# Two store waits of SyncE moved from ahead of the program's closing barrier to behind it

## The chip, the cores and the metric

The kernel runs on one core of one Trainium2 chip. The metric is the device time of one execution in microseconds (us), lower is better. Each execution also gives its **span**, from the first to the last instruction of the program, rounded to 0.1 us. The time is longer than the span in every run here, by 1.24 to 2.17 us, so it also contains something outside the program. I take that to be the runtime's work around it. I call time minus span the **excess**. I call the stretch from the issue of the last store to the end of the span the **tail**.

## The reference, cut to what matters

```python
def _A_ref(x, k_cache, v_cache, wq, wo):        # 32 heads, 32768 keys each
    q = ...(x @ wq)...
    scores = einsum("bhqd,bhkd->bhqk", q, k_cache) * Dh ** -0.5
    o = einsum("bhqk,bhkd->bhqd", softmax(scores), v_cache)
    return ...o... @ wo                          # 512 values
def _B_ref(...):                                 # 8 kv heads, only the last 4096 keys; the same otherwise
    ...
return concatenate([a, b], axis=-1)              # (1, 1, 1024) bf16
```

One token attends over two caches. The kernel reads 570 MB and writes two rows of 1 KB. B's row is ready early, A's row is the last thing to be made.

## The kernel before: the parts concerned

Instructions are collected as a list per engine (`self.op(engine, ...)`) and emitted in one block. Leaving the block emits a barrier of all five engines. In the trace of the kernel before, the drains of TensorE, VectorE, ScalarE and SyncE there each update one semaphore, SyncE's last (its end: 1321.126 us). GpSimd's next record waits for that semaphore (1321.151) and its last one updates a second (1321.230); the records of the other four that wait for the second start at 1321.271 to 1321.283.

```python
def build(self):
    ...
    with nc.Block() as block:                    # line 101: its end is the closing barrier
        block.gpsimd(self.emit("pool"))
        block.vector(self.emit("dve"))
        block.scalar(self.emit("act"))
        block.sync(self.emit("sp"))
        block.tensor(self.emit("pe"))

def plan(self):
    ...                                          # loads, B, 32 heads of A, output weights
    self.emit_proj()
    for n in self.outsem:                        # SyncE's last instructions
        self.op("sp", lambda e, n=n: e.wait_ge(self.outsem[n], 16))

def emit_proj(self):
    ...
    self.op("sp", lambda e: e.dma_start(self.out[0, :, 512:1024], self.qrow[0:1, :])
            .then_inc(self.outsem["B"], 16), o)               # line 740, the first store
    ...
    self.op("sp", lambda e: e.dma_start(self.out[0, :, 0:512], self.out_sb[:, :])
            .then_inc(self.outsem["A"], 16), *done)           # line 755, the last store
```

A wait for a store is kept in every kernel here: the landing comes 1.09 us after the issue's start. What happens without a wait, no run shows. Each store has a semaphore of its own (`outsem`), and a wait is for its count of 16.

## Time and profile before

| kernel before | us |
|---|---|
| median of its first three runs (range) | 1323.31 (1323.26 to 1323.33) |
| span of the profiled run | 1321.3 |
| last output copy ends, on VectorE | 1319.76 |
| last store issued (start, end) | 1319.845, 1320.093 |
| landing of that store, as its semaphore's last update records it (the wait ends 17 ns after) | 1320.937 |
| end of the block's barrier, end of the span | 1321.334 |

The page and the views that lead there are shown in the prediction below. Times to the nanosecond are taken from the trace's own records of the same instructions, which the views round to 0.1 us. The records also hold each update of a semaphore.

### The profile page before, as it was taken

To read this page: it belongs to the slowest core of one execution; us is meant where nothing else is said; L and a number is where in the kernel's file an instruction comes from. 1 tells how busy PE (TensorE), PEld (TensorE's weight loads), DVE (VectorE), ACT (ScalarE), POOL (GpSimd) and SP (SyncE) were. 2 spreads that over 40 slices of the span, in tenths; PEclk is the share of its full clock that TensorE was granted. 3 is DMA by queue.
4 is the path that set the end of the run, shared out by engine and by line. 5 is a ranking of instruction groups with operands and counts; after the bars stand their busy time and mean duration, and the time that the engine had idled before them with its cause. 6 is when DMAs were issued, how large, how long until landed. Compare 5 with 4: busy or idle time off the path is not lost. (4 is left out here: it accounts for less than half of the span.)

```text
span 1321.3 us, 28784 instructions
## 1 busy us (share of the span) xinstructions
PE 967.9 (73%) x13243; PEld 675.8 (51%) x13243; DVE 752.0 (57%) x1341; ACT 55.2 (4%) x168; POOL 2.6 (0%) x22
## 2 busy tenths in 40 slices
PE   4675678776777878676787767678776777877787
PEld 3453445554444655444465544455554445555453
DVE  3663556665455666554566655466655556665563
ACT  0000000000000000000000000000000000000000
POOL 0000000000000000000000000000000000000000
PEclk8886888888789888878988887898878779887898
DMA  9999999999999999999999999999999999999998
GB/s 403 434 438 428 442 433 429 440 436 427 439 436 429 438 438 427 436 438 433 431 438 434 429 438 434 429 438 436 427 440 432 431 440 432 429 440 434 431 436 367
DMA packets 13359, 570.59 MB, mean 432 GB/s; under 512 B 1570, under 2 KB 1700, under 8 KB 2084
## 3 DMA queue, kind: packets, MB, share of 16 engines
q1 hardware_dynamic: 13060, 570.43, 99.8%
q8 instruction: 8, 0.13, 0.0%
q10 hardware_dynamic: 288, 0.00, 0.0%
q14 instruction: 3, 0.02, 0.0%
HBM read 570.43 MB, written 0.00 MB: 432 GB/s over the span
## 5 line engine op out<-in xcount | busy, mean ns | idle before, releaser
L557 DVE COPY kt<-psT 128x1024 bf16<-128x1024 bf16 x1056 | 655.6, 684 | 237.0 <-PE psT L553 235.2
L553 PE MATMUL psT<-ident,kbuf 128*128 128x128 bf16 x8448 | 580.6, 234 | 167.3 <-DMA kbuf<-in_A_k_cache_dram 152.9
L553 PEld LDWEIGHTS psT<-ident,kbuf 128*128 128x128 bf16 x8448 | 540.7, 106 | 259.8 <-DMA kbuf<-in_A_k_cache_dram 161.0
L656 PE MATMUL psACC<-vbuf,ptsb 128*4 128x512 bf16 (+1 forms) x2112 | 183.9, 524 | 22.8 <-ACT ptsb L631 22.0
L576 PE MATMUL psS<-kt,qw 128*32 128x512 bf16 x2048 | 158.3, 386 | 15.0 <-DVE kt L557 15.0
L670 DVE TENSOR_SCALAR oc_A<-psACC,hot_A 128x128 f32<-128x128 f32 x32 | 11.2, 351 | 248.5 <-PE psG L683 248.5
L656 PEld LDWEIGHTS psACC<-vbuf,ptsb 128*4 128x4 bf16 (+1 forms) x2112 | 59.7, 110 | 137.4 <-issue 89.6
L604 ACT ACTIVATE psb<-psS,nb_A 128x512 bf16<-128x512 f32 x32 | 22.0, 687 | 1165.5 <-DVE nb_A L603 1165.5
L576 PEld LDWEIGHTS psS<-kt,qw 128*32 128x32 bf16 x2048 | 34.1, 95 | 57.8 <-DVE kt L557 31.2
L683 PE MATMUL psG<-oc_A,hw 128*32 128x128 f32 (+1 forms) x128 | 19.3, 227 | 52.3 <-DVE oc_A L672 52.3
L683 PEld LDWEIGHTS psG<-oc_A,hw 128*32 128x32 f32 x128 | 11.4, 109 | 62.5 <-DVE oc_A L672 55.1
L628 PE MATMUL psPT<-ident,psb 128*128 128x128 bf16 x136 | 18.0, 275 | 34.0 <-ACT psb L604 34.0
L672 DVE SCALAR_TENSOR_TENSOR oc_A<-psACC,hot_A,oc_A 128x128 f32<-128x128 f32 x96 | 33.7, 351 | 3.4
L593 DVE TENSOR_REDUCE tr_in<-psS 128x1 f32<-128x512 f32 x34 | 23.5, 692 | 17.6 <-PE psS L576 17.6
L628 PEld LDWEIGHTS psPT<-ident,psb 128*128 128x128 bf16 x136 | 10.1, 117 | 37.0 <-ACT psb L604 36.7
L597 PE MATMUL psACC<-rows,tr_in 128*1 128x64 f32 x64 | 8.8, 220 | 25.6 <-DVE tr_in L593 25.6
L631 ACT ACTIVATE ptsb<-psPT 128x512 bf16<-128x512 bf16 x34 | 20.3, 597 | 31.0 <-PE psPT L628 31.0
L597 PEld LDWEIGHTS psACC<-rows,tr_in 128*1 128x1 f32 x64 | 2.7, 81 | 35.5 <-DVE tr_in L593 35.5
L601 PE MATMUL psACC<-mr_A,nscale 1*128 1x1 f32 x64 | 12.4, 260 | 9.8 <-DVE mr_A L600 9.8
L601 PEld LDWEIGHTS psACC<-mr_A,nscale 1*128 1x128 f32 x64 | 9.7, 188 | 15.8 <-DVE mr_A L600 15.8
L603 DVE COPY nb_A<-psACC 128x1 f32<-128x1 f32 x32 | 5.0, 157 | 15.3 <-PE psACC L601 15.3
L495 PE MATMUL psACC<-vbuf,x_B 128*2 128x512 bf16 x32 | 3.6, 627 | 13.7 <-DMA x_B<-in_B_x_dram 13.7
(82 smaller groups left out, 76.0 us busy)
## 6 DMA issues: line engine op xcount, KB each, us to landing
kbuf<-in_A_k_cache_dram SPq DMA_DIRECT2D x4, 4096.0 KB, 22.4
kbuf<-in_B_k_cache_dram SPq DMA_DIRECT2D x2, 4096.0 KB, 31.8
vbuf<-in_B_v_cache_dram SPq DMA_DIRECT2D x2, 4096.0 KB, 24.7
vbuf<-in_B_wq_dram SPq DMA_DIRECT2D x1, 4096.0 KB, 12.7
vbuf<-in_A_wq_dram SPq DMA_DIRECT2D x1, 4096.0 KB, 32.2
kbuf<-in_B_wo_dram SPq DMA_DIRECT2D x2, 2048.0 KB, 33.6
kbuf<-in_A_wo_dram SPq DMA_DIRECT2D x1, 1408.0 KB, 28.0
kbuf<-in_A_wo_dram SPq DMA_DIRECT2D x1, 1024.0 KB, 30.1
```

Source lines behind the costliest of these rows:

```text
L553: inst = e.transpose(T[:, 128 * k:128 * k + 128], src[:, DH * k:DH * k + DH], self.ident[:, :])
L557: self.copies.append(self.op("dve", lambda v: v.tensor_copy(KT[:, :], T[:, :]), o, to="pe"))
L576: inst = e.matmul(self.S[32 * c:32 * c + 32, :], lhsT=win, rhs=self.kt[(bb + c // 2) % NKT][:, 512 * (c % 2):512 * (c % 2) + 512], start=b ...
L593: o = dve(lambda v: v.reduce_max(tr["in"][:, 0:1], self.S[:, :], axis=AXX), self.sdone, self.k_pool, to="pe" if name == "A" else None)
L597: o = self.op("pe", lambda e: e.matmul(self.ACC[0:1, 0:64], lhsT=tr["in"][:, 0:1], rhs=self.rows64[:, :], start=True, stop=True, skip_grou ...
L601: o = self.op("pe", lambda e: e.matmul(self.ACC[:, 64:65], lhsT=self.nscale[:, :], rhs=t["mr"][0:1, :], start=True, stop=True, skip_group_ ...
L604: self.sread = self.op("act", lambda s: s.activation(out=self.psb[:, :], in_=self.S[:, :], func=ACTF.Exp, bias=t["nb"][:, k:k + 1], scale= ...
L628: inst = e.transpose(PT[:, 128 * jj:128 * jj + 128], self.psb[:, 128 * jj:128 * jj + 128], self.ident[:, :])
L631: self.ptread = self.op("act", lambda s: s.activation(out=self.ptsb[:, :], in_=PT[:, 0:512], func=ACTF.Copy), self.psread, to="pe")
L656: inst = e.matmul(acc[32 * c:32 * c + rows, 0:512], lhsT=lhsT, rhs=rhs, start=begin, stop=end, tile_position=(0, 32 * c), skip_group_check ...
L672: o = self.op("dve", lambda v, src=src, hot=hot: v.scalar_tensor_tensor(out=oc, in0=src, scalar=hot, in1=oc, op0=ALU.mult, op1=ALU.add), p ...
L683: return self.op("pe", lambda e: e.matmul(self.G[0:32, c0 + c:c0 + c2], lhsT=win, rhs=t["oc"][g % len(t["oc"])][:, c:c2], start=False, sto ...
```

## The change

The intent is to let the closing barrier run while the last store is still in flight. SyncE issues the store, takes part in the barrier at once, and only then waits.

```diff
@@ build
             block.sync(self.emit("sp"))
             block.tensor(self.emit("pe"))
+        for n in self.X:
+            nc.sync.wait_ge(self.outsem[n], 16)
@@ plan
         self.emit_proj()
-        for n in self.outsem:
-            self.op("sp", lambda e, n=n: e.wait_ge(self.outsem[n], 16))
```

## The prediction

> **What bounds the kernel now.** I read the page from the top down, then its last five microseconds. The slices come first, since they show which resource limits most of the run.
>
> ```profile
> DMA  9999999999999999999999999999999999999998
> ...
> DMA packets 13359, 570.59 MB, mean 432 GB/s; under 512 B 1570, under 2 KB 1700, under 8 KB 2084
> ```
>
> Every slice but the last has its 16 DMA engines at least 90% busy, while TensorE stands at 73% and VectorE at 57% of the span. The kernel streams 570.59 MB and nothing on an engine matters before the stream ends. The change touches no load and nothing that starts a load, so some 1319 us of the 1321.3 us span should come out as before. Only the tail is at stake, so next is the end of the chain of work that ended last (start us, us, what).
>
> ```profile
> 1285.36 31.48 DMA kbuf<-in_A_wo_dram
> 1316.83 0.04 issue
> 1316.88 2.45 PE psPT L719 x29
> 1319.33 0.02 issue
> 1319.35 0.41 DVE out_sb L726
> ```
>
> The last weights land, TensorE finishes the projection, VectorE copies the row out at 1319.76. The remaining 1.57 us of the span hold no busy engine: they are the store of that row and the barrier. SyncE's waits show how they divide (what it waited for; us in total, times, longest).
>
> ```profile
> SPq L182 <- ACT out_sb L727: 6.3, 1, 6.3
> SPq L101 <- DMA out_dram<-out_sb: 0.8, 1, 0.8
> ...
> SPq L101 <- PEq L101: 0.2, 1, 0.2
> ```
>
> SyncE sits 0.8 us for the landing of the second store (out_sb), then meets the barrier of the block (line 101). The first store (qrow) costs nothing: it was issued at 1313.16, and its own wait passed at 1320.1 without delay. The instructions of line 101 in the last 7 us (op, count, duration in ns, first and last start) give the barrier:
>
> ```profile
> L101 POOLq EVENT_SEMAPHORE  x2: 17/17/17, 1321.2 to 1321.2; - x2
> L101 PEldq DRAIN  x1: 355/355/355, 1319.0 to 1319.0; - x1
> L101 DVEq DRAIN  x1: 451/451/451, 1319.4 to 1319.4; - x1
> L101 ACTq DRAIN  x1: 404/404/404, 1319.4 to 1319.4; - x1
> L101 SPq COMPARE_BRANCH  x1: 33/33/33, 1321.0 to 1321.0; - x1
> L101 SPq DRAIN  x1: 7/7/7, 1321.1 to 1321.1; - x1
> L101 SPq EVENT_SEMAPHORE  x1: 17/17/17, 1321.3 to 1321.3; - x1
> ...
> L101 PEldq EVENT_SEMAPHORE  x1: 51/51/51, 1321.3 to 1321.3; - x1
> ```
>
> TensorE, VectorE and ScalarE had drained by 1319.8. All of them, and GpSimd, wait for SyncE's drain at 1321.1, which stands behind the landing. So landing and barrier are in series, and both are on the path that ends the span.
>
> To the nanosecond, from the trace's own records of the instructions that these views round: store issued 1319.845 to 1320.093; wait for the first store 1320.145; branch, carrying the wait for the second store, released at 1320.954; SyncE's drain 1321.119; GpSimd's two semaphore steps 1321.151 and 1321.230; SyncE's step 1321.271; TensorE's step 1321.283, 51 ns long, which ends the span at 1321.334.
>
> [...] the issue took 0.25 us, the landing was seen 1.11 us after its start (1320.954 - 1319.845). [...] this SyncE store shows 1.11 us, and I use that. [...] the time exceeds the span by 2.15 us in the profiled run (1323.45 - 1321.3)[...].
>
> **The change part by part.** It removes two waits from SyncE's body and adds the same two, in the order A then B, behind the block. No transfer, copy or matmul is added or dropped. Step by step:
>
> 1. Up to the end of the store's issue, 1320.093, nothing changes.
> 2. The branch no longer carries the landing. It follows the issue at the distance at which the wait for the first store now does (52 ns): 1320.145, instead of 1320.954. It is 0.81 us earlier.
> 3. The drain follows the branch by 165 ns as now: 1320.310.
> 4. The rest follows the drain as now: SyncE's step by 152 ns (1320.462), TensorE's end by 215 ns (1320.525). The barrier is over 0.43 us before the landing, so it is wholly hidden.
> 5. SyncE then waits for store A. Its landing is untouched, so the wait is released at 1320.954. The record of a wait is 17 ns long (as at 1320.1), and the next one starts 57 ns after (the distance of the last wait and the issue behind it, 1319.788 and 1319.845). Store B is long there: its wait starts at 1321.011 and ends at 1321.028.
>
> The new end is 1321.03 instead of 1321.33: **0.31 us saved**, the 0.38 us of branch, drain and barrier behind the landing (1321.334 - 1320.954) less the 0.07 us of two wait records. Taken from the median of 1323.31 us that gives 1323.00, if what follows the span keeps its length. The gain is the shorter of the two things now side by side, not the 0.8 us of the wait.
>
> **The rivals.** First, *the drain swallows the wait*. If SyncE's drain waits for its outstanding transfers, the barrier stays behind the landing and two wait records come on top: about 1323.4. The opening barrier speaks against it. SyncE issues two 4096 KB loads ahead of that barrier's drain, and its drain and semaphore step were (the lines of the opening barrier, then the load from its issue to landing):
>
> ```profile
> L768 SPq DRAIN  x1: 120/120/120, 0.9 to 0.9; - x1
> L768 SPq EVENT_SEMAPHORE  x1: 17/17/17, 1.2 to 1.2; - x1
> ```
> ```profile
> vbuf<-in_B_wq_dram SPq DMA_DIRECT2D x1, 4096.0 KB, 12.7
> ```
>
> The drain took 120 ns with a load in flight that landed at 12.7 us. So it does not wait for landings. It may have waited for the issue just before it (its start is 53 ns after that issue's end); in the new tail the branch puts 217 ns between the two. If it still grew to 120 ns, it would only eat into the 0.43 us of slack.
>
> Second, *the other four engines' early release is worth more*. They pass the barrier some 0.8 us earlier (1320.5 instead of 1321.3). If what the runtime does after the kernel is long on one of those engines and not tied to SyncE, the time falls by up to that 0.8 us: 1322.5. [...] It gets about a quarter of the weight.
>
> Third, *the landing sets the end anyway and the barrier was never exposed*: if the time ended with SyncE's landing and not with the barrier, nothing would move, 1323.3. The order of the records (landing, then drain, then the four steps) speaks against it. [...]
>
> **Range and chances.** The central figure is 1323.0 us: the sum gives 1323.00, and the second rival pulls down as much as the first and third pull up. The three runs of before differ by 0.07 us, but another build of a stream-bound program may shift by a few tenths for reasons outside the change, an allowance of mine. Low end 1322.4 (a little below the second rival's 1322.5), high end 1323.5 (first rival plus that). 2% is 26 us, and the whole tail behind the last copy is 1.57 us, so only a disturbance could leave the band: 0.99 for within 2%.
>
> **What would show it.** Right: in the changed kernel's trace the branch of SyncE starts about 52 ns after the issue, the four engines' steps of line 101 lie near 1320.5, before the store's landing, and the last record is SyncE's own wait, about 0.3 us earlier in the span than now. SyncE's 0.8 us wait is replaced by a wait of about 0.4 us for the same landing. Step 3 is wrong if the drain's record is long or comes after the landing; step 5 if the landing itself moved. If the span falls by 0.3 us and the time by clearly more or less, the runtime's part after the span is what I mis-sized. The prediction as a whole is wrong if the stream before 1319 us comes out different, since nothing in the change accounts for that.

The sum stays 1323.31 - 0.31 = 1323.00 us. For the second rival, its quarter of the weight is an estimate of mine alone.

## More of the kernel before

All runs here were in the fast state. No run of any kernel was set aside.

## The result, and the profile after

| | before | after |
|---|---|---|
| median time, six runs each (range) | 1323.73 (1323.26 to 1324.39) | 1322.70 (1322.46 to 1323.53) |
| ratio of the times (95% interval) | | 0.9993 (0.998 to 1.0006) |
| tail of the profiled run | 1.489 | 1.114 |
| excess, mean (range); 32 runs of before beside the experiments, six of after | 2.11 (2.04 to 2.16) | 1.71 (1.66 to 1.76) |

The ratio is the mean time of one kernel's fast runs over that of the other's runs of the same rounds, so it is not quite the ratio of the medians. Its interval includes 1. By the time alone, nothing is shown: the 32 runs of the kernel before that stood beside the experiments lie between 1323.12 and 1324.59 us, and their spans between 1321.0 and 1322.5 us. That scatter comes from the 1319 us ahead of the last store, which both kernels share. The profiled run of the changed kernel shows it: its last output copy starts at 1320.05 us, 0.70 us later than before (1319.35), so its span is longer although its tail is shorter. The end of its chain of work shows where (start us, us, what):

```profile
1314.73 2.27 PE psT L741 x11
1317.01 3.02 PE psPT L719 x42
1320.03 0.02 issue
1320.05 0.41 DVE out_sb L726
```

Before, this chain came from a weight load. Here its 45 us run over engines, mostly TensorE and VectorE, and hold no transfer. Of the fourteen traces, six end like before, with the copy at 1319.10 to 1319.48 us, and eight like this one, with the copy at 1319.75 to 1321.77 us. Both endings occur with the wait ahead of the barrier (before and e3 below) and behind it. What decides between them, no run here shows.

The tail and the excess do not contain that scatter. (The tail and the steps below come from one trace per kernel, the excess from every run.) The tail is 0.375 us shorter, the excess 0.40 us. **Together the change saves 0.78 us**, about 0.06% of the time.

SyncE's last waits in the changed kernel (what it waited for; us in total, times, longest):

```profile
SPq L184 <- ACT out_sb L727: 4.7, 1, 4.7
SPq L108 <- DMA out_dram<-out_sb: 0.4, 1, 0.4
...
SPq L101 <- PEq L101: 0.2, 1, 0.2
```

The wait for the landing stands on line 108 now, behind the barrier, and has shrunk from 0.8 to 0.4 us: the other 0.4 us of the same flight are filled by the barrier. The barrier's instructions and the wait, by source line (op, count, duration in ns, first and last start):

```profile
L101 POOLq EVENT_SEMAPHORE  x2: 17/17/17, 1321.1 to 1321.2; - x2
...
L101 SPq DRAIN  x1: 206/206/206, 1320.9 to 1320.9; - x1
L101 SPq EVENT_SEMAPHORE  x1: 17/17/17, 1321.2 to 1321.2; - x1
...
L101 PEldq EVENT_SEMAPHORE  x1: 51/51/51, 1321.2 to 1321.2; - x1
```
```profile
L108 SPq EVENT_SEMAPHORE  x1: 373/373/373, 1321.3 to 1321.3; - x1
```

Three things differ from what I had laid out. There is no branch record of SyncE on line 101 any more; its drain follows the issue's end after 58 ns. The drain is 206 ns long instead of 7. And one wait record carries both stores' semaphores, where I had counted two. The barrier ends at 1321.265; the landing comes at 1321.636, 1.091 us after the issue's start (1.092 before; 1.09 to 1.10 in all fourteen traces). The span ends 23 ns later.

SyncE's drain ended at 1321.057, while the trace has the store's packet move only from 1321.262 on. So this drain did not wait for the transfer.

**What lies behind the span.** All that follows is read from the profiler's own records. No instruction of the program waits for semaphore 2 or updates it, and yet the trace has it stepped 18 times after the last block barrier, in both kernels. Between the sixth and the tenth of these steps 246 other semaphores, numbered from 7 on, are updated once each, all within 0.69 us (677 to 1363 ns behind the span) in the kernel before, and 247 within 0.66 us in the changed one. I call the 18 steps the **closing steps**. The expectations below call them steps of the runtime's closing barrier: that the runtime makes them, and that they are a barrier, is my reading, and no trace names them. Here are these steps, in ns from the end of the span, and the landing of the last store (L) among them:

```text
before:  L -397 |  241  275  485  528  552  651 ...  1826 1864 1898 1945
after:           -123  -89 | L -23 |  91  135  158  257 ...  1406 1444 1478 1525
```

In the changed kernel two of these steps (-123 and -89 ns) were taken while SyncE still waited for the landing (-23 ns). From landing to last step it takes 2.342 us before and 1.548 us after: 0.79 us less, the tail's and the excess's gain in one number. Who took the two steps, and what sets the third, was open. That is what the experiments are about.

### The profile page after: what moved, and what is told of

Read it like the earlier page. It is cut to its first block, busy times and chain, and to the rows that moved or that the text cites. A ratio compares the mean times of both kernels' runs of the same rounds, so it can differ in the third digit from the quotient of the medians.

```text
span 1321.7 us, 28783 instructions
## 1 busy us (share of the span) xinstructions
PE 968.2 (73%) x13243; PEld 673.7 (51%) x13243; DVE 750.7 (57%) x1341; ACT 55.1 (4%) x168; POOL 2.6 (0%) x22
## 5 line engine op out<-in xcount | busy, mean ns | idle before, releaser
L656 PE MATMUL psACC<-vbuf,ptsb 128*4 128x512 bf16 (+1 forms) x2112 | 187.0, 531 | 22.8 <-ACT ptsb L631 22.0
L600 DVE TENSOR_REDUCE mr_A<-psACC 1x1 f32<-1x64 f32 x32 | 6.8, 213 | 11.7 <-PE psACC L597 11.7
```

What stands on the lines that cost most here:

```text
L656: inst = e.matmul(acc[32 * c:32 * c + rows, 0:512], lhsT=lhsT, rhs=rhs, start=begin, stop=end, tile_position=(0, 32 * c), skip_group_check ...
```

## The experiments

My theory after the result: 0.38 us of the gain is the block's barrier hidden behind the landing, and 0.40 us is the head of the closing steps, which the four other engines can now begin early. The first rival: the excess shrank for some other reason, such as the code at the end of SyncE's stream. All kernels below gave correct results. The expectations count the tail from the end of the store's issue, which is 0.25 us less than in my tables (1.24 for 1.49, 0.87 for 1.11), and take the changed kernel's excess as 1.69 us.

### Every engine held (e1_all_wait)

```diff
-        for n in self.X:
-            nc.sync.wait_ge(self.outsem[n], 16)
+        for e in (nc.sync, nc.gpsimd, nc.vector, nc.scalar, nc.tensor):
+            for n in self.X:
+                e.wait_ge(self.outsem[n], 16)
```

> All five engines, not SyncE alone, wait for the two stores behind the block's barrier. Theory: of the roughly 0.8 us that the tail lost, 0.38 us is the block's barrier hidden behind the landing and some 0.42 us is the head of the runtime's own closing barrier, which the four engines enter while SyncE still waits. Then this kernel keeps the short span (issue of the last store to end of span about 0.87 to 0.95 us, as in the changed kernel, not 1.24 us) but loses the second part: the time exceeds the span by about 2.1 us again, as before, not by 1.7 us. Rival: the part behind the span got shorter for another reason, such as other code at the end of SyncE's stream; then the excess stays near 1.7 us here.

The waits of the five engines behind the barrier, by source line:

```profile
L109 POOLq EVENT_SEMAPHORE  x1: 416/416/416, 1320.6 to 1320.6; - x1
L109 SPq EVENT_SEMAPHORE  x1: 379/379/379, 1320.6 to 1320.6; - x1
...
L109 PEldq EVENT_SEMAPHORE  x1: 312/312/312, 1320.7 to 1320.7; - x1
```

All sit 0.3 to 0.4 us for the landing. The tail is 1.13 us, short as in the changed kernel; the excess is 2.15 us (2.13 to 2.17, four runs), long as before. The first closing step comes 0.24 us behind the landing, none ahead of it. So the two gains are separable, and the second one is the early release of engines that have nothing to wait for. The rival (excess 1.7) falls.

### Each half alone (e2_a_behind, e3_b_behind)

```diff
 # e2: in SyncE's body                      # e3: in SyncE's body
-        for n in self.outsem:              -        for n in self.outsem:
+        for n in ("B",):                   +        for n in ("A",):
 # e2: behind the block                     # e3: behind the block
+        for n in ("A",):                   +        for n in ("B",):
+            nc.sync.wait_ge(...)           +            nc.sync.wait_ge(...)
```

> Half the change: only the wait for the last store (A) moves behind the barrier, the wait for the first store (B), which landed long ago, stays in SyncE's body. Theory: B's wait costs nothing where it stands, so this is as fast as the full change: excess of the time over the span 1.7 us, issue of the last store to end of span about 0.87 us. SyncE's drain, 206 ns long in the changed kernel because it stands directly behind the issue, starts some 57 ns later behind B's wait and is shorter by about as much or back at a few ns; the barrier ends before the landing either way. Rival (both waits had to leave the body, since a branch stays there that carries a wait): a branch and its 165 ns come back, and the barrier ends later, but still ahead of the landing.

> The other half: the wait for the last store (A) stays ahead of the barrier, only B's wait is behind it. Theory: nothing is gained, because what counts is what stands behind the landing of the last store. Landing, branch, drain and barrier stay in series, and one wait record that is already fulfilled comes on top: issue of the last store to end of span 1.24 us or up to 0.07 us more, excess over the span within 0.1 us of 2.1 us. Rival (moving any wait shortens SyncE's body and with it the tail): 0.2 us or more is gained.

With only A's wait behind the barrier, the tail is 1.13 us and the excess 1.65 us (four runs): the whole gain. SyncE's part of the barrier there:

```profile
L101 SPq COMPARE_BRANCH  x1: 38/38/38, 1320.8 to 1320.8; - x1
L101 SPq DRAIN  x1: 36/36/36, 1321.0 to 1321.0; - x1
```

The branch record is back, 38 ns long and carrying B's wait, as that rival had it: here as in before (33 ns), e3 and e6, a wait is the last thing in SyncE's body and is carried by a branch record. The drain, starting 0.23 us behind the issue's end, is only 36 ns long; in the changed kernel it starts 58 ns behind it and takes 206 ns, in before 1.03 us behind it and takes 7 ns. In these three traces its length goes with the distance from the issue just before it. The branch and the shorter drain cancel: in both kernels the barrier ends 0.72 us after the issue's start, ahead of the landing.

With only B's wait behind it, the wait is fulfilled on arrival:

```profile
L108 SPq EVENT_SEMAPHORE  x1: 17/17/17, 1322.4 to 1322.4; - x1
```

Tail 1.53 us, 0.04 us longer than before; excess 2.03 us, 0.08 us less than before, within what I had allowed. The two sum to a gain of 0.04 us, where the full change has 0.78. Moving B's wait is worth nothing.

### Another engine waits (e5_wait_act, e5_wait_pool, e5_wait_dve, e5_wait_pe)

```diff
-            nc.sync.wait_ge(self.outsem[n], 16)
+            nc.scalar.wait_ge(self.outsem[n], 16)      # or gpsimd, vector, tensor
```

> ScalarE, not SyncE, waits for the two stores behind the barrier. Theory: the runtime's closing barrier is a chain from engine to engine. In the changed kernel's trace two steps of it (updates of its semaphore, 0.12 and 0.09 us before the end of the span) were already made while SyncE waited, and the next came 0.09 us after the span. An engine later in that chain than SyncE would let more of it pass during the landing and bring the excess of the time over the span below 1.69 us, down to some 1.5 us; one earlier would let less pass and bring it up to 2.1 us. I do not know ScalarE's place; the number of steps that the trace shows before the landing tells it. Rival (only SyncE's being held matters, whoever waits): the excess is 1.69 us for every engine that waits, within 0.05 us. The span stays short, 0.87 to 0.95 us from the issue of the last store.

> GpSimd waits behind the barrier, with no other engine waiting. Same reading as with ScalarE: excess 1.5 us if GpSimd stands late in the runtime's chain, up to 2.1 us if it stands first; 1.69 us for all four by the rival. Of all four waiters, two should stand ahead of SyncE's place (excess above 1.7 us) and two behind it (below)[...].

> VectorE waits behind the barrier. Same reading: excess between 1.5 and 2.1 us by its place in the runtime's chain, 1.69 us by the rival; short span as in the changed kernel.

> TensorE waits behind the barrier. Same reading: excess between 1.5 and 2.1 us by its place in the runtime's chain, 1.69 us by the rival; its wait record is 51 ns long where the other engines' are 17 to 21, so the span may be some 0.03 us longer than with SyncE.

The tail is 1.12 to 1.13 us in all four. The rest, with the changed kernel as the SyncE row (closing steps in ns from the end of the span; the step that the held engine delays is marked):

| who waits | steps ahead of the landing | next steps | excess, mean |
|---|---|---|---|
| TensorE | 0 | **231**, 265, 303, 346, 370 | 1.93 |
| ScalarE | 1 | **131**, 169, 213, 236 | 1.78 |
| GpSimd | 2 | **542**, 586, 610 | 2.14 |
| VectorE | 2 | 74, **159**, 183 | 1.76 |
| SyncE | 2 | 91, 135, 158 | 1.71 |

The rival (1.69 for everyone) falls, and so does my guess that two engines stand ahead of SyncE and two behind. All four stand ahead: the order in these traces is TensorE, ScalarE, GpSimd, VectorE, SyncE. Holding GpSimd makes the third step late, by 0.54 us after its wait ends; holding TensorE, ScalarE or VectorE delays the first, second or fourth (to 231, 131 and 159 ns). That SyncE is the fifth is shown by the kernel without a block below, where four steps come ahead of the landing. So the change picked the right engine: holding any other gives back 0.05 to 0.43 us of the excess. VectorE's 0.05 us is hardly clear of the spread of single runs (1.71 to 1.80 us, SyncE's 1.66 to 1.76).

The table holds something more. In SyncE's row nothing holds GpSimd, and yet the third step comes 0.114 us after the landing. Measured from GpSimd's last record in the block's barrier to the third step, it is 0.572 us in the kernel before, in the changed kernel, in e2, in e3 and in e5_wait_dve alike. So there were two new theories. **G**: GpSimd's 0.57 us way from the block's barrier to its closing step is what bounds the tail now, and the landing itself is hidden. **L**: the landing bounds.

### A longer barrier (e6_before_bar1, e7_after_bar1, e8_after_bar3)

```diff
             block.tensor(self.emit("pe"))
+        nc.all_engine_barrier()          # e6 on before, e7 on after, e8 on after three times
```

> The kernel before with a second barrier of all engines behind the block's, both behind the landing. It sizes one barrier where nothing hides it. Both theories: the span's tail (issue of the last store to end of span) grows from 1.24 us by 0.2 to 0.3 us (drain to SyncE's step took 0.15 us in the block's barrier, and the drain comes some 0.05 us behind the step before), the excess of the time over the span stays at 2.10 us.

> The changed kernel with that second barrier between the block's and the waits, so ahead of the landing. Theory L (the landing bounds the tail, the barrier hides behind it): the barrier ends at least 0.1 us before the landing is seen, so the span's tail stays at 0.87 us, and at most the 0.09 us that GpSimd's step came late is added. Theory G (new, from the traces so far: the first step of the runtime's closing barrier behind TensorE's and ScalarE's comes 0.57 us after GpSimd leaves the block's barrier in every kernel but those where another waiter is later, so GpSimd's way from the block's barrier bounds the tail, and the landing has already become the hidden one by about 0.1 us): the span stays at 0.87 us, but the excess grows by the barrier's whole 0.2 to 0.3 us, from 1.69 to 1.9 or 2.0 us. Both agree on the span; the excess tells them apart.

> The changed kernel with three more barriers ahead of the waits, 0.6 to 0.9 us in all. The barriers outlast the landing by some 0.25 to 0.5 us; SyncE's waits find both stores landed and are 17 to 20 ns long. Nothing is hidden behind the landing any more: the excess is back at 2.0 to 2.1 us, and the span's tail is 1.15 to 1.45 us. If the excess stayed at 1.7 us, theory G and the account by the early release would both be wrong.

| | tail | excess, mean of four | landing to third step | landing to last step |
|---|---|---|---|---|
| before | 1.489 | 2.11 (32 runs) | 0.882 | 2.342 |
| before + 1 barrier (e6) | 1.829 | **1.72** | 1.204 | 2.639 |
| after | 1.114 | 1.71 (six runs) | 0.114 | 1.548 |
| after + 1 barrier (e7) | 1.111 | **1.65** | 0.438 | 1.874 |
| after + 3 barriers (e8) | 1.745 | 2.09 | 1.086 | 2.915 |

A barrier in the open costs 0.34 us (e6's tail less before's), somewhat over my 0.2 to 0.3. Ahead of the landing it does not lengthen the tail at all, as both theories had it. The wait for the landing is then all but over on arrival, 45 ns long (e7):

```profile
L109 SPq EVENT_SEMAPHORE  x1: 45/45/45, 1322.1 to 1322.1; - x1
```

But the two measures of what follows now disagree. By the closing steps, e7 loses 0.33 us against the changed kernel, the barrier's whole cost, as G says. By the excess it loses nothing, as L says. And e6, whose steps behind the span are within 0.04 us of before's, has an excess of 1.72 us where 2.10 was expected. The expectation for e6 is a plain miss. Something takes about 0.35 us off the excess of e6 and e7 that shows in no closing step. What the two share is that each engine's stream is two or three instructions longer.

e8 hit the number (2.0 to 2.1 us), with its wait 28 ns long and its tail 0.3 us above what I allowed, since the three extra barriers took 0.99 us. But it is a poor witness: its sixth closing step comes 0.50 us behind the fifth, where before has 0.10, and that extra 0.4 us would fill up what e6 and e7 had lost. Gaps of that size also stand ahead of the last four steps in e1 and in the kernel in which VectorE waits, without any trace of them in the excess. So the time does not end simply with the last of these steps, and I do not lean on e8.

### No block at all (e9_no_block)

```diff
-        with nc.Block() as block:
-            block.gpsimd(self.emit("pool"))
-            ...
+        for eng, e in (("pool", nc.gpsimd), ("dve", nc.vector), ("act", nc.scalar), ("sp", nc.sync), ("pe", nc.tensor)):
+            self.emit(eng)(e)
```

> The changed kernel without the block: each engine's instructions stand in the main program, so there is no closing barrier at all, and SyncE alone waits for the stores. GpSimd is done within the first 5 us and reaches the runtime's barrier at once. Theory G: GpSimd's step no longer bounds, so the tail is bound by SyncE and the landing; the steps behind the landing come at once: excess below 1.69 us by up to 0.1 us, 1.6 us. Theory L (the landing already bounds in the changed kernel): excess 1.69 us, nothing gained. The span's tail is 0.87 us by both (landing plus 0.02 us). The time is 0.8 to 0.95 us below that of before, near the limit of what so few runs can show.

Without the block there is no closing barrier in the program, and SyncE's wait is the only thing behind its last store:

```profile
L104 SPq EVENT_SEMAPHORE  x1: 814/814/814, 1321.3 to 1321.3; - x1
```

Tail 1.115 us as expected. Four closing steps lie ahead of the landing, the fifth comes 0.134 us after it (0.181 in the changed kernel), the last 1.446 us after it (1.548): 0.10 us earlier, what G expected. About half of that is there at the fifth step, the rest from the sixth on. The excess is 1.25 us (1.24 to 1.26, five runs), which is 0.35 us lower than G's 1.6. So a third kernel whose streams have another length (eleven recorded instructions fewer, where e6 and e7 have eleven more) shows the same unexplained third of a microsecond.

### Longer streams, nothing else (e10_after_pad)

```diff
+        for e, n in ((nc.gpsimd, 3), (nc.vector, 2), (nc.scalar, 2), (nc.sync, 2), (nc.tensor, 2)):
+            for _ in range(n):
+                e.drain(fusable=False)
         with nc.Block() as block:
```

> The changed kernel with as many extra instructions as one more barrier has (three drains on GpSimd, two on each other engine), but ahead of the block, where the engines wait for the first load anyway. The tail is that of the changed kernel, only the code behind it lies as many instructions further on in each engine's stream. Open question: with a second barrier ahead of the landing the runtime's steps came 0.33 us later, as theory G said, but the excess of the time over the span stayed at 1.66 us, as theory L said; and before with a second barrier had an excess of 1.72 instead of 2.10 us at unchanged runtime's steps. Theory P: the length of the streams alone takes 0.35 to 0.4 us off what follows the runtime's last steps; then the excess here is 1.3 to 1.4 us, the runtime's steps stay as in the changed kernel (third step 0.07 to 0.1 us behind the span), and G holds after all, the barrier's cost and P's gain having cancelled. Rival L: GpSimd's way does not bound the time, the number of instructions does not matter: excess 1.69 us here. The span's tail stays at 0.87 us by both, and the time should be about 1.2 us below that of before by P, 0.8 us by L.

The padding runs at the very start, where every engine waits for the first load:

```profile
L103 POOLq DRAIN  x3: 34/34/41, 1.2 to 1.4; - x3
L103 SPq DRAIN  x2: 7/7/7, 1.3 to 1.3; - x2
```

The tail (1.119 us), the third step (0.109 us after the landing) and the last (1.542) are those of the changed kernel (1.114, 0.114, 1.548). The excess is 1.35 us (1.31 to 1.38, five runs), against 1.71. **Padding alone takes 0.36 us off**, as P had it, and its rival falls. With that term known, e7's excess is the changed kernel's 1.71 less 0.36 plus the barrier's 0.33, that is 1.68 against the measured 1.65: G holds, and the barrier's cost and the padding's gain had cancelled. In the same way e6 should have 2.11 less 0.36, that is 1.75, against 1.72.

What the padding changes physically stays open, and so does where it acts. None of the recorded steps moves, and the padded kernel's excess, 1.35 us, is shorter than the 1.52 us from the end of its span to the last step, so the effect cannot simply be placed behind that step. Take the excess less that stretch for each kernel: it is +0.14 to +0.19 us in before, in the changed kernel, in e2, in e3 and with ScalarE, GpSimd or TensorE waiting, and -0.17 to -0.20 us in e6, e7, e9 and here (the three kernels with an odd gap, e1, e8 and the one in which VectorE waits, are left out). That is one jump of about 0.36 us, for eleven instructions more as for eleven fewer, so P's "length of the streams" is not a matter of more being faster. The traces also record transfers of instructions: only e8's has one behind the span (8 KB, 1.60 us behind it), so no recorded one sets the padded kernel apart. I did not vary the padding engine by engine. Before and the changed kernel differ by one recorded instruction, and the changed kernel's gain shows in the closing steps (0.42 us from the end of the span) as well as in the excess (0.40 us). So this effect is no part of the 0.78 us.

Of the fourteen kernels, the one without a block has the lowest tail and excess, 2.36 us together (1.115 + 1.25), then the padded one with 2.47 (1.119 + 1.35); the changed kernel has 2.82, before 3.60. Their times were 1322.64 and 1322.18 us in the median, beside 1323.74 and 1323.66 of before in the same rounds, with ratios of 0.9989 (0.9976 to 1.0003) and 0.9990 (0.9977 to 1.0004): the intervals still include 1.

## Why the prediction was right or wrong

The median of 1322.70 us lies in the range, and the change is within 2%. The scatter of the time is larger than the effect, so the agreement of the time proves little; the steps must be judged by the trace.

- **Step 1 and the bound.** Nothing ahead of the last store changed by design, and the store's flight is the same to 1 ns. Right for the change. But "nothing on an engine matters before the stream ends" is too strong a reading: in eight of the fourteen traces the last chain ends on engines and not on a load.
- **Step 2, the branch.** It did not move 0.81 us ahead, it vanished from the record. In these traces it is there where a wait is the last thing in SyncE's body (33 ns in before, 38 ns in e2; also in e3 and e6).
- **Step 3, the drain.** Sized at 7 ns, with 120 ns named as the case that would only eat slack. It took 206 ns, and it did only eat slack: with no branch between, it stands directly behind the issue (58 ns after its end).
- **Step 4, the hidden barrier.** Right. It ended 0.47 us after the issue's end (0.43 predicted) and 0.37 us ahead of the landing.
- **Step 5, the waits.** One record instead of two, and the span ends 23 ns behind the landing's update where I had some 90. So the tail lost 0.375 us instead of 0.31.
- **The step that failed** is the condition on which the sum stood: "if what follows the span keeps its length". It did not, and the sign that the prediction gave for this (the time falls by clearly more than the span's part) came true. The excess fell by 0.40 us, a term as large as the whole predicted saving, which the sum sets to zero. In its place e1 showed that the four other engines' early release carries this part: hold them too and the excess is back at 2.15 us. Holding GpSimd alone does as much (2.14 us).
- **The rivals.** The second rival named this mechanism and its size, "up to that 0.8 us", close to the 0.78 us found, and got a quarter of the weight. What I held against it rested on no trace. The runs answer it: without a block four closing steps come while SyncE still waits, and its own is the fifth, 0.134 us after the landing (e9). The first rival (the drain swallows the wait) fell: the drain ended 0.2 us before the store's packet moved. The third fell, as the tail did get shorter, by 0.375 us. What e10 did show, 0.36 us less with eleven padding instructions more, is not part of this change's gain.
- **"The gain is the shorter of the two things now side by side."** True inside the span. It was too narrow, because three things now run side by side: the landing, the block's barrier, and the way of the other engines to their closing steps. With G shown, GpSimd's way is the longest, by 0.05 us over SyncE's own at the fifth step (0.181 us behind the landing, against 0.134 without a block) and 0.10 us at the last. G also gives the gain in one figure: GpSimd's last record in the block's barrier ends 0.633 us after the last store's issue begins, where before it ended after 1.402 us. That is 0.77 us earlier, as good as the whole 0.78 us.

## What to carry to other kernels

In this kernel the wait that protects only the end of the program did best behind everything that does not need it, on one engine alone (on all five the excess is 2.15 us), and on SyncE, whose closing step comes behind those of the other four (1.71 us, against 1.76 with VectorE, hardly apart, and 1.78 to 2.14 with the others). Elsewhere, test the same. Look for what the other engines can do meanwhile beyond the end of the span too, since the metric contains it: here 0.40 of the 0.78 us. When an effect is smaller than the scatter of the time, split the time into a part that carries the scatter and parts that carry the change, and before crediting a few tenths of a microsecond to a removed or added instruction, test what the same number of instructions does elsewhere in the stream.
